# Attention in units of eight heads on two row tiles of the array, with only own blocks of q loaded and the first group written as one list

## The chip, the cores and the metric

The kernel runs on one core of a Trainium2 chip. The metric is the device time of one execution in microseconds. Three timed runs of the kernel before gave 860.01 us in the median (857.99 to 861.16). Chances are told against 0.5% of that, 4.3 us, about what a measurement of this kernel can tell from no change.

## The reference

Three stages follow one another, all in float32.

```python
# attention: B, H, S, D = 4, 8, 576, 64
scores = q @ k.T / 8
# heads 0..3: 0 <= i - j < 32;  heads 4..7: 0 <= i - j < 128 and (i - j) % 4 == 0; else -1e9
attn = softmax(scores);  x = attn @ v            # then x becomes 2304 tokens x 512
# first MLP, d_ff = 2048
h = x @ w_in;  x = (h - tanh(h)) @ w_out
# second MLP, d_ff = 1024
x = (((x @ w1) * (x @ w2)) @ w3) @ w_out
```

A dilated head is a plain window of 32 once its tokens are sorted by their place modulo four, so all heads have a window of 32 keys, and a block of 32 queries needs 64 keys.

## The kernel before, in words

**Numbers.** Weights come from the host as 64-bit floats and are turned into float32 on the chip: one load on SP's queue (L100, tile `st`), `Abs` on ACT (L105), four VectorE instructions on the bits (L110, L114, L120, L123), then a high part on ACT (L128) and a low part on GpSimd (L129). This is called the conversion of a weight below. `tick()` does one step of such a pipeline. The large products are three passes of high and low parts (`mm3`, L415, and `st_y`, L492).

**Attention.** A unit is one batch, one type (plain or dilated), and one of three stretches of 192 queries: 24 units of four heads, two pairs of heads in each. The host lays q out as `qz`: for each pair of heads 128 rows, where a block's 128 columns hold the 64 queries of the first head in the upper 64 rows, those of the second in the lower 64 rows, and zeros elsewhere. So one product over 128 rows gives the scores of one head, though half of its rows are zeros. A unit goes through these steps: `load_q` (one DMA for k, one for q), `load_v` (two DMAs, or four in the first stretch), `at_scores` (one bf16 product that writes the mask, L283, then 24 products in four column tiles of 32, L293), `at_max` and `at_norm` on VectorE, `at_exp` on ACT, the scaling by the sum on GpSimd (L318), three transposes (`at_T`, L326), two copies into a block-diagonal buffer `pb` (L333), `at_pv` (12 products of 64 moving columns, L353), and the high and low part of the result in X (L369, L370).

**First MLP.** The 16 blocks of d_ff are worked off in groups of 3, 4, 4 and 5. In a group, a step is one block for one tile of tokens: `st_h`, tanh on ACT (L449), `h - tanh(h)` on VectorE (L455), its high part on ACT (L457) and low part (L464, on GpSimd in the first group, on VectorE later), and in the next step `st_y`, whose four results are added to Y (L503, L505, L507). In the first group six tiles of 256 tokens and two of 384 are used, later four of 512 and one of 256.

**Order.** Each engine works off its instructions in the order in which the program issues them. `start_up` does the attention of the first batch (six units), with 24 warming products ahead and one per unit. After that, `attn_slot` does one more step of the attention's pipeline for every 1.33 (first six steps) or 1 steps of the first group, so that its products stand between those of the MLP. Every DMA of the attention and of the weights is issued by SP, in one row, and the program gives the DMAs eight semaphores in turn, so that an issue waits until the transfer eight places ahead of it has landed.

The conversions of a group's weights stand in the steps by `tick()`: after the step's VectorE work and after the sums into Y.

Of the kernel before, what the change touches and what calls it, by code (L numbers as in the profile page):

```python
# [15 lines left out]
PS, PT, PX, TE, PH = 2, 1, 2, 2, 1  # L16
GS = (3, 4, 4, 5)
RF = 1.0
WU, WC = 24, 512
NW, NL = 16, 18  # L20
TS = [512] * 4 + [256]
TC, GP, YE = 3, 1, 2
# [14 lines left out]
NB_P = 2  # L37
# [6 lines left out]
KC = DM // 128  # L44


@with_exitstack
def attn_moe_kernel(
# [78 lines left out]
    def cv_split(a, hi, lo):  # L127
        nc.scalar.activation(out=hi, in_=a.bitcast(F32), func=ACTF.Copy)  # L128
        nc.gpsimd.tensor_tensor(out=lo, in0=a.bitcast(F32), in1=hi.bitcast(F32), op=ALU.subtract)  # L129


    W = {}
    queue = deque()
    for c in range(NFC):
        queue.append((("in", c), w_in[c]))
        queue.append((("out", c), w_out[c]))
# [18 lines left out]
    def tick():  # L155

        if bitsed:
            key, a = bitsed[0]
            if len(free) - (reserve[0] if key[0] in ("w1", "w2") else 0) >= 2:
                bitsed.popleft()  # L160
                hi, lo = free.popleft(), free.popleft()
                cv_split(a, hi, lo)
                W[key] = (hi, lo)
        if absed and not bitsed:
            key, st, a = absed.popleft()
            cv_bits(st, a)
            bitsed.append((key, a))
        prefetch()
        if loaded and not absed:
            key, st = loaded.popleft()  # L170
            absed.append((key, st, cv_abs(st)))

# [14 lines left out]
    units = [(b, ty, g) for b in range(B) for ty in (0, 1) for g in range(NG)]  # L187
    PB = 2 * NG
# [5 lines left out]
    def open_attn():  # L194
        st = ExitStack()
        attn_pools["stack"] = st
        one = st.enter_context(tc.tile_pool(name="att", bufs=1))
        attn_pools["pb"] = one.tile([128, NB_P, TU, 4, 2, HQ], F32, name="pb")
        attn_pools["kv"] = st.enter_context(tc.tile_pool(name="kv", bufs=3))
        attn_pools["pp"] = st.enter_context(tc.tile_pool(name="pp", bufs=3))  # L200
        attn_pools["sm"] = st.enter_context(tc.tile_pool(name="sm", bufs=4))
        attn_pools["psS"] = st.enter_context(tc.tile_pool(name="psS", bufs=PS, space=PSUM))
        attn_pools["psT"] = st.enter_context(tc.tile_pool(name="psT", bufs=PT, space=PSUM))
        attn_pools["psX"] = st.enter_context(tc.tile_pool(name="psX", bufs=PX, space=PSUM))

        for e in range(2):
            nc.gpsimd.memset(attn_pools["pb"][64 * e:64 * e + 64, :, :, :, 1 - e], 0.0)
        m = one.tile([128, 6, HW], F32, name="m")
        for j in range(4):
            r = slice(HQ * j, HQ * j + HQ)  # L210
            nc.scalar.dma_start(out=m[r, 1:], in_=masks[r, 1:, 32 * (j % 2):32 * (j % 2) + HW])
        nc.scalar.dma_start(out=m[:, 0], in_=masks[:, 0, :HW])
        nc.scalar.dma_start(out=id_sb, in_=ident)
        attn_pools["m"] = m

    def prep_masks():
        m = attn_pools["m"]

        def put(to, src, eng):
            shape = [128, (to.stop - to.start - 1) // (to.step or 1) + 1, HW]  # L220
            if src.shape[1] != shape[1]:
                src = src.to_broadcast(shape)
            if eng:
                nc.scalar.activation(out=mask_sb[:, to], in_=src, func=ACTF.Copy)
            else:
                nc.vector.tensor_copy(out=mask_sb[:, to], in_=src)

        nc.vector.tensor_copy(out=id16_sb, in_=id_sb)
        put(slice(9, 10), m[:, 0:1], 0)
        put(slice(10, 13), m[:, 1:2], 0)  # L230
        put(slice(0, 1), m[:, 0:1], 1)
        put(slice(1, 6, 2), m[:, 1:2], 1)
        put(slice(2, 7, 2), m[:, 2:5], 1)
        put(slice(7, 8), m[:, 5:6], 1)
        put(slice(8, 9), m[:, 1:2], 1)
# [8 lines left out]
    def load_q(n):  # L244
        if n < len(units):
            b, ty, g = units[n]
            k0, k1 = KS[TU * g], KS[TU * g + TU - 1] + KW
            k = attn_pools["kv"].tile([128, 2, TU * QT + 32], F32, tag="k", name="k")
            nc.sync.dma_start(
                out=k[:, :, :k1 - k0], in_=kT[b, 2 * ty:2 * ty + 2, :, k0:k1].rearrange("e p k -> p e k")  # L250
            )
            q = attn_pools["kv"].tile([128, 2, TU, 2 * QT], F32, tag="q", name="q")
            nc.sync.dma_start(
                out=q, in_=qz[b, 2 * ty:2 * ty + 2, :, TU * g:TU * g + TU].rearrange("e p t c -> p e t c")
            )
            ks[n] = k, q
# [5 lines left out]
    def load_v(n):  # L262
        if n < len(units):
            b, ty, g = units[n]
            v = attn_pools["kv"].tile([128, 2, TU, 2 * D], F32, tag="v", name="v")
            for e in range(2):

                for t0, t1 in ((0, 1), (1, TU)) if g == 0 else ((0, TU),):
                    src = vt[b, 2 * ty + e, :HW, TU * g + t0:TU * g + t1].rearrange("k t c -> k (t c)")
                    ap = [list(d) for d in src.ap]  # L270
                    step = ap[0][0] * window(TU * g + t0, 1)
                    nc.sync.dma_start(
                        out=v[64 * e:64 * e + 64, :, t0:t1].rearrange("k h t c -> k h (t c)"),
                        in_=bass.AP(tensor=src.tensor, offset=src.offset, ap=[ap[0], [step, 2], ap[1]]),
                    )
            vs[n] = v

    def at_scores(n):
        b, ty, g = units[n]
        k, q = ks.pop(n)  # L280
        ps = attn_pools["psS"].tile([128, TU, 2, HW], F32, tag="s", name="s")
        m0 = (M_DIL if ty else M_PLAIN)[g]
        nc.tensor.matmul(  # L283
            out=ps, lhsT=id16_sb,
            rhs=mask_sb[:, m0:m0 + TU].unsqueeze(2).to_broadcast([128, TU, 2, HW]),
            start=True, stop=False, skip_group_check=True,
        )
        for i in range(TU):
            t = TU * g + i
            for e in range(2):  # L290
                for j in range(4):
                    k0 = KS[t] - KS[TU * g] + window(t, j % 2)
                    nc.tensor.matmul(  # L293
                        out=ps[HQ * j:HQ * j + HQ, i, e], lhsT=q[:, e, i, HQ * j:HQ * j + HQ],
                        rhs=k[:, e, k0:k0 + HW], start=False, stop=(i == TU - 1),
                        skip_group_check=True, tile_position=(0, HQ * j),
                    )
        ms = attn_pools["sm"].tile([128, 2, 2 * TU], F32, tag="ms", name="ms")
        ust[n] = dict(ps=ps.rearrange("p i e k -> p (i e) k"), mx=ms[:, 0], sm=ms[:, 1])

    def at_max(n):
        s = ust[n]
        nc.vector.tensor_reduce(out=s["mx"], in_=s["ps"], axis=AX.X, op=ALU.max)
        s["pm"] = attn_pools["pp"].tile([128, 2 * TU, HW], F32, tag="pm", name="pm")
        nc.vector.tensor_tensor(
            out=s["pm"], in0=s["ps"], in1=s["mx"].unsqueeze(2).to_broadcast([128, 2 * TU, HW]), op=ALU.subtract
        )

    def at_exp(n):
        s = ust[n]  # L310
        nc.scalar.activation(out=s["pm"], in_=s["pm"], func=ACTF.Exp, scale=0.125)

    def at_norm(n):
        s = ust[n]
        nc.vector.tensor_reduce(out=s["sm"], in_=s["pm"], axis=AX.X, op=ALU.add)
        nc.vector.tensor_scalar(out=s["sm"], in0=s["sm"], scalar1=1e-9, scalar2=None, op0=ALU.add)
        nc.vector.reciprocal(out=s["sm"], in_=s["sm"])
        nc.gpsimd.tensor_tensor(  # L318
            out=s["pm"], in0=s["pm"], in1=s["sm"].unsqueeze(2).to_broadcast([128, 2 * TU, HW]), op=ALU.mult
        )  # L320

    def at_T(n):
        s = ust[n]
        pt = attn_pools["psT"].tile([128, TU, 128], F32, tag="t", name="t")
        for i in range(TU):
            nc.tensor.transpose(pt[:, i], s["pm"][:, 2 * i:2 * i + 2].rearrange("p a k -> p (a k)"), id_sb)  # L326
        s["ptp"] = pt

    def at_Tcopy(n):
        s = ust[n]  # L330
        pb = attn_pools["pb"][:, n % NB_P]
        for e in range(2):
            nc.scalar.activation(  # L333
# [37 lines left out]

    LAGN, LAGT, LAGP = 1, 2, 3
    slot = [0]
    first = [0] * 4

    def attn_slot():

# [15 lines left out]
        if on[0]:  # L393
            at_max(n)
# [409 lines left out]
```

## Time and profile before

| | us |
|---|---|
| median of three runs | 860.01 |
| the profiled execution, whole | 861.07 |
| its span, first to last instruction | 859.3 |
| TensorE busy (share of the span) | 819.1 (95%) |
| VectorE busy | 483.9 (56%) |
| ScalarE busy | 293.8 (34%) |
| GpSimd busy | 133.0 (15%) |

The profiled execution is 1.8 us longer than its span, and 1.1 us above the median. The span falls into stages: up to about 40 us the attention of the first batch; then the first group of the first MLP with the other three batches' attention between its steps, up to 174.46 us, where the first product of the second group stands; then the other groups of the first MLP (up to about 511 us) and the second MLP. Matmuls are pipelined, so a busy TensorE is not one at its peak; start-to-start times of its blocks say what a block costs.

### The profile page before, as it was taken

What the parts mean: (1) busy time and instruction counts of PE and PEld (TensorE: products, weight loads), DVE (VectorE), ACT (ScalarE), POOL (GpSimd) and SP (SyncE); (2) the same over time, 40 slices, a digit from 0 to 9 for tenths busy, and PEclk for the clock granted to TensorE, in tenths of its full rate; (3) what the DMA queues carried; (4) which work ended last, traced back from release to release, by engine and by line L of the source; (5) the groups of instructions that cost most, each with busy time, mean ns of one, the idle gap of its engine ahead of it and who ended that gap; (6) DMA issues with size and microseconds to landing.
All of it is one profiled execution on the core that took longest, in us unless ns stands there. A gap on an engine that the chain in (4) does not pass through costs nothing.

```text
span 859.3 us, 13590 instructions
## 1 busy us (share of the span) xinstructions
PE 819.1 (95%) x5568; PEld 688.7 (80%) x5574; DVE 483.9 (56%) x789; ACT 293.8 (34%) x557; POOL 133.0 (15%) x120
## 2 busy tenths in 40 slices
PE   7588999999999999999999979999999999999998
PEld 4477999877789788888888878886788888888897
DVE  5588654888735873378888885577612212222121
ACT  3545655444422432234343333333311211211121
POOL 2243232222100210012211131222100000000000
PEclk9789999999999999999999999999999999999999
DMA  9978851222300320012322322133010010010010
GB/s 258 270 216 237 231 169 39 74 99 98 99 1 6 107 84 1 1 50 99 98 74 74 99 98 73 50 99 109 14 50 1 0 50 1 1 49 1 1 50 25
DMA packets 36511, 67.74 MB, mean 79 GB/s; under 512 B 4320, under 2 KB 24928, under 8 KB 36448
## 3 DMA queue, kind: packets, MB, share of 16 engines
q1 hardware_dynamic: 35456, 66.60, 25.5%
q8 instruction: 44, 0.72, 0.3%
q10 hardware_dynamic: 992, 0.26, 0.1%
q14 instruction: 19, 0.16, 0.1%
HBM read 62.13 MB, written 4.72 MB: 78 GB/s over the span
## 4 chain that ended last, share of the span: by engine, by line
PE 65%; DVE 21%; DMA 6%; ACT 5%; issue 2%; SPq 0%; ACTq 0%; DVEq 0%
PE h L415 37%; PE y L492 14%; PE o L697 10%; DVE a L110 4%; DVE a L114 3%; DVE a L120 3%; DVE a L123 3%; DVE th L455 2%; DVE gs L464 2%; ACT gs L457 2%; DMA st<-in_w 2%; PE x L353 2%; DMA v<-in_vt 2%; PE s L293 1%; DVE Y L507 1%
## 5 line engine op out<-in xcount | busy, mean ns | idle before, releaser
L415 PE MATMUL h<-X,LT 128*128 128x512 f32 (+1 forms) x576 | 131.3, 368 | 0.0
L492 PE MATMUL y<-gs,WG 128*128 128x256 f32 (+2 forms) x648 | 123.3, 338 | 5.0 <-DVE Y L507 3.0
L415 PE MATMUL h<-WG,X 128*128 128x512 f32 (+1 forms) x441 | 120.3, 375 | 0.0
L492 PEld LDWEIGHTS y<-gs,WG 128*128 128x128 f32 x648 | 102.4, 189 | 20.2 <-ACT WG L128 2.2
L415 PEld LDWEIGHTS h<-X,LT 128*128 128x128 f32 x576 | 101.5, 188 | 18.0
L415 PE MATMUL h<-X,WG 128*128 128x256 f32 (+2 forms) x567 | 113.9, 341 | 2.1 <-ACT X L369 1.2
L678 DVE TENSOR_TENSOR a_sb<-h,a_sb 128x512 f32<-128x512 f32 (+1 forms) x40 | 25.5, 638 | 158.5 <-PE h L415 152.3
L415 PEld LDWEIGHTS h<-X,WG 128*128 128x128 f32 x567 | 91.8, 196 | 11.7 <-ACT X L369 1.5
L492 PE MATMUL y<-gs,LT 128*128 128x512 f32 (+1 forms) x420 | 93.9, 373 | 5.7 <-ACT gs L457 4.6
L415 PEld LDWEIGHTS h<-WG,X 128*128 128x128 f32 x441 | 83.2, 189 | 15.2
L492 PEld LDWEIGHTS y<-gs,LT 128*128 128x128 f32 x420 | 74.4, 192 | 20.4 <-ACT gs L457 5.6
L455 DVE TENSOR_TENSOR th<-h,th 128x512 f32<-128x512 f32 (+2 forms) x89 | 52.1, 585 | 66.4 <-ACT th L449 66.3
L105 ACT ACTIVATE a<-st 128x512 f32<-128x512 f32 x72 | 48.5, 673 | 100.4 <-DMA st<-in_w 48.6
L457 ACT ACTIVATE gs<-th 128x512 fp32r<-128x512 f32 (+2 forms) x89 | 49.0, 550 | 92.9 <-DVE th L455 92.9
L449 ACT ACTIVATE th<-h 128x512 f32<-128x512 f32 (+2 forms) x89 | 45.4, 510 | 76.3 <-PE h L415 75.9
L464 DVE TENSOR_TENSOR gs<-th,gs 128x512 fp32r<-128x512 f32 (+2 forms) x71 | 44.9, 632 | 46.2 <-ACT gs L457 45.2
L415 PE MATMUL h<-LT,X 128*128 128x512 f32 (+1 forms) x198 | 60.6, 375 | 0.0
L114 DVE TENSOR_SCALAR a<-a 128x512 uint32<-128x512 uint32 x72 | 58.0, 805 | 2.5
L110 DVE TENSOR_SCALAR a<-a 128x512 f32<-128x512 f32 x72 | 59.0, 819 | 0.5 <-ACT a L105 0.5
L129 POOL TENSOR_TENSOR X<-a,X 128x512 fp32r<-128x512 f32 x26 | 35.6, 1367 | 130.5 <-ACT X L128 119.0
L123 DVE SCALAR_TENSOR_TENSOR a<-st,a 128x512 uint32<-128x512 uint32 x72 | 54.2, 753 | 2.5
L120 DVE SCALAR_TENSOR_TENSOR a<-st,a 128x512 uint32<-128x512 uint32 x72 | 53.6, 744 | 2.4
(69 smaller groups left out, 990.3 us busy)
## 6 DMA issues: line engine op xcount, KB each, us to landing
st<-in_w SPq DMA_DIRECT2D x32, 512.0 KB, 3.4
q<-in_qz SPq DMA_DIRECT2D x24, 384.0 KB, 5.1
st<-in_w_in SPq DMA_DIRECT2D x16, 512.0 KB, 3.5
st<-in_w_out SPq DMA_DIRECT2D x16, 512.0 KB, 3.5
v<-in_vt SPq DMA_DIRECT2D x32, 192.0 KB, 5.3
st<-in_wo SPq DMA_DIRECT2D x8, 512.0 KB, 3.4
k<-in_kT SPq DMA_DIRECT2D x16, 224.0 KB, 5.2
v<-in_vt SPq DMA_DIRECT2D x16, 128.0 KB, 3.6
```

Source lines behind the costliest of these rows:

```text
L105: nc.scalar.activation(out=a.bitcast(F32), in_=st[:, :, 1].bitcast(F32), func=ACTF.Abs)
L110: nc.vector.tensor_scalar(out=a.bitcast(F32), in0=a.bitcast(F32), scalar1=2.0 ** -15, scalar2=CMAX, op0=ALU.max, op1=ALU.min,)
L114: nc.vector.tensor_scalar(out=a, in0=a, scalar1=3, scalar2=0x3FFFFFFF, op0=ALU.logical_shift_left, op1=ALU.bitwise_and,)
L120: nc.vector.scalar_tensor_tensor(out=a, in0=st[:, :, 1], scalar=0xC0000000, in1=a, op0=ALU.bitwise_and, op1=ALU.bitwise_or)
L123: nc.vector.scalar_tensor_tensor(out=a, in0=st[:, :, 0], scalar=29, in1=a, op0=ALU.logical_shift_right, op1=ALU.bitwise_or)
L415: nc.tensor.matmul(out=ps, lhsT=a[sel[0]], rhs=b[sel[1]], start=(i == 0), stop=(i == n - 1), **kw)
L449: nc.scalar.activation(out=th[:, :tn], in_=gst[i][:, :tn], func=ACTF.Tanh)
L455: nc.vector.tensor_tensor(out=th[:, :tn], in0=ps[:, :tn], in1=th[:, :tn], op=ALU.subtract)
L457: nc.scalar.activation(out=gs[:, 0, :tn], in_=th[:, :tn], func=ACTF.Copy)
L464: eng.tensor_tensor(out=gs[:, 1, :tn], in0=th[:, :tn], in1=gs[:, 0, :tn].bitcast(F32), op=ALU.subtract)
L492: nc.tensor.matmul(out=y[k], lhsT=wt[sel[0]][:, 128 * k:128 * k + 128], rhs=gs[:, sel[1], :tn], start=(c == 0 and n == 0 and (not packed o ...
L697: nc.tensor.matmul(out=ps, lhsT=cs[:, e, 128 * m:128 * m + 128], rhs=WW[j][f], start=(j == 0 and n == 0), stop=(j == NJ - 1 and n == 2),)
```

## The change

A unit now has eight heads: both types of a batch and stretch together, 12 units in all. The four heads of the plain type lie on rows 0 to 63 of k and q, those of the dilated type on rows 64 to 127. `load_q` fetches k with one DMA of 64 rows per type, and of q only the blocks that are not zero, with four DMAs of 64 rows per type, in pieces of 64 numbers. `at_scores` puts the type on a row tile of the array (`tile_position=(64 * ty, ...)`), and each type writes a bank of its own. `at_pv` takes the transposed weights as they are, without the block-diagonal buffer: 24 products of 32 moving columns per type in four tiles of 64 x 64 instead of 12 of 64 columns. Max, subtraction, exp and sum go over both types in one instruction from the second batch on. In the first batch the types are worked on apart, and its tiles lie in Y, which is not needed yet.

The attention and the whole first group (eight tiles: seven of 256 tokens, one of 512) stand in one list of words, `ORDER`: a letter for the step, a number for the unit, weight or MLP step, p or d for one type. `q`, `v`, `w` are loads, `s` scores, `T` transposes, `P` the products with v, `h` and `y` those of the MLP, `a b c i o` a conversion. The list holds the conversions of all eight weights of the second group too. In the later groups two blocks of the tile of 256 tokens share one step, and `tick()` stands between the high and the low part of a step, ahead of the low part and of the sums into Y.

```diff
+ORDER = """
+q0p S10 v2p K0 q2p K1 s0p w0 S5 M0p q1p E0p s2p N0p q0d S3 a0 m0p M2p T0p b0 E2p q1d C0p s1p N2p c0
...
-    units = [(b, ty, g) for b in range(B) for ty in (0, 1) for g in range(NG)]
-    PB = 2 * NG
+    units = [(b, g) for b in range(B) for g in range(NG)]
+    PB = NG
...
-            nc.sync.dma_start(
-                out=q, in_=qz[b, 2 * ty:2 * ty + 2, :, TU * g:TU * g + TU].rearrange("e p t c -> p e t c")
-            )
+            for ty in parts:
+                r = slice(64 * ty, 64 * ty + 64)
+                nc.sync.dma_start(
+                    out=k[r, :, :k1 - k0],
+                    in_=kT[b, 2 * ty:2 * ty + 2, :, k0:k1].rearrange("e (h p) k -> p (e h) k", h=2),
+                )
+                for m in range(4):
+                    e, h = divmod(m, 2)
+
+                    nc.sync.dma_start(
+                        out=q[r, e, h],
+                        in_=qz[b, 2 * ty + e, D * h:D * h + D, TU * g:TU * g + TU, QT * h:QT * h + QT],
+                    )
...
+                for ty in parts:
+                    r = slice(64 * ty, 64 * ty + 64)
+                    for j in range(4):
+                        h, half = divmod(j, 2)
+                        k0 = KS[t] - KS[TU * g] + window(t, half)
+                        nc.tensor.matmul(
+                            out=ps[ty][HQ * j:HQ * j + HQ, 2 * i + e],
+                            lhsT=q[r, e, h, i, HQ * half:HQ * half + HQ],
+                            rhs=k[r, 2 * e + h, k0:k0 + HW], start=False, stop=(i == TU - 1),
+                            skip_group_check=True, tile_position=(64 * ty, HQ * j),
+                        )
...
-                nc.tensor.matmul(
-                    out=dst, lhsT=v[:, half, i, D * h:D * h + D],
-                    rhs=pb[:, i, j].rearrange("p a q -> p (a q)"), start=True, stop=True,
-                )
...
+                            nc.tensor.matmul(
+                                out=dst, lhsT=v[64 * e:64 * e + 64, half, i, D * h:D * h + D],
+                                rhs=s["pt"][ty][64 * e:64 * e + 64, i, HQ * j:HQ * j + HQ],
+                                start=True, stop=True, tile_position=(64 * e, 64 * h),
+                            )
...
-        sizes = [256] * 6 + [384] * 2 if g == 0 else TS
+        sizes = TS if g else TS0
...
+            w = 2 if g and tn == 256 else 1
...
+        for i in range(N0, NS + 1):
             if i < NS:
...
+                if i > N0:
+                    settle()
+                    st_h(i)
+                    st_tanh(i)
+                    st_g(i)
+                    st_ghi(i)
+                tick()
+                if i > N0:
+                    st_glo(i)
+            if i > N0:
+                st_y(i - 1)
+                st_evac(i - 1, 0)
+                st_evac(i - 1, 1)
```

Three places show how the order moves. First SP's row of DMA issues, in the middle of the attention: before, a stretch with three loads of k and q, of four heads each.

```order
L249 DMA k<-in_kT 128x2x192
L253 DMA q<-in_qz 128x2x384
L272 DMA v<-in_vt 64x2x128
L272 DMA v<-in_vt 64x2x256
L272 DMA v<-in_vt 64x2x128
L272 DMA v<-in_vt 64x2x256
L249 DMA k<-in_kT 128x2x224
L253 DMA q<-in_qz 128x2x384
L272 DMA v<-in_vt 64x2x384 x2
L249 DMA k<-in_kT 128x2x224
L253 DMA q<-in_qz 128x2x384
```

And now, the loads of unit 10 (k and q of both types) and of v for the dilated type of unit 6, which the list puts right behind them.

```order
L121 DMA st<-in_w_out 128x1024
L306 DMA k<-in_kT 64x4x224
L313 DMA q<-in_qz 64x3x64 x4
L306 DMA k<-in_kT 64x4x224
L313 DMA q<-in_qz 64x3x64 x4
L333 DMA v<-in_vt 64x2x128
L333 DMA v<-in_vt 64x2x256
L333 DMA v<-in_vt 64x2x128
L333 DMA v<-in_vt 64x2x256
```

Four heads took one issue for k and one for q; they now take one and four, and all of them move 64 rows instead of 128.

Second TensorE, in the middle of the first group: before, one slot of the attention between two steps of the MLP.

```order
L415 MATMUL h<-X,WG 128x256 x12
L492 MATMUL y_1095<-gs,WG 128x256 x6
L492 MATMUL y_1096<-gs,WG 128x256 x6
L353 MATMUL x<-pb,v 64x2x32 x12
L283 LDWEIGHTS id_sb
L283 MATMUL s<-mask_sb,id_sb 128x384
L293 MATMUL s<-k,q 32x64 x24
L326 MATMUL t<-id_sb,pm 128x128 x3
L415 MATMUL h<-X,WG 128x256 x12
```

And now, `y9 P7 s10 T8d h11` of the list.

```order
L609 MATMUL y_1892<-gs,WG 128x256 x6
L476 MATMUL x<-p,v 64x8x4 x24
L476 MATMUL x<-p,v 64x32 x24
L389 LDWEIGHTS id_sb
L389 MATMUL s<-mask_sb,id_sb 128x384
L389 LDWEIGHTS id_sb
L389 MATMUL s<-mask_sb,id_sb 128x384
L402 MATMUL s<-k,q 32x64 x48
L447 MATMUL t<-id_sb,pm 128x128 x3
L519 MATMUL h<-X,WG 128x256 x12
```

The products with v stand for both types at once and are twice as many; the scores of both types stand in one block of 48.

Third VectorE in the second group, around the end of a tile: before.

```order
L455 TENSOR_TENSOR th<-h,th 128x512
L464 TENSOR_TENSOR gs<-th,gs 128x512
L507 TENSOR_TENSOR Y<-y_3310,Y 128x256
L507 TENSOR_TENSOR Y<-y_3311,Y 128x256
L507 TENSOR_TENSOR Y<-y_3312,Y 128x256
L507 TENSOR_TENSOR Y<-y_3313,Y 128x256
L110 TENSOR_SCALAR a<-a 128x512
L114 TENSOR_SCALAR a<-a 128x512
L120 SCALAR_TENSOR_TENSOR a<-st,a 128x512
L123 SCALAR_TENSOR_TENSOR a<-st,a 128x512
```

And now.

```order
L567 TENSOR_TENSOR th<-h,th 128x512
L131 TENSOR_SCALAR a<-a 128x512
L135 TENSOR_SCALAR a<-a 128x512
L141 SCALAR_TENSOR_TENSOR a<-st,a 128x512
L144 SCALAR_TENSOR_TENSOR a<-st,a 128x512
L581 TENSOR_TENSOR gs<-th,gs 128x512
L627 TENSOR_TENSOR Y<-y_3679,Y 128x512
L627 TENSOR_TENSOR Y<-y_3680,Y 128x512
L627 TENSOR_TENSOR Y<-y_3681,Y 128x512
L627 TENSOR_TENSOR Y<-y_3682,Y 128x512
```

The four instructions of a conversion moved from behind the sums into Y to a place between the step's difference (`th`) and its low part (`gs`).

## Rows read from the trace of the kernel before

**Rows 1.** Windows: length, busy time of each engine, clock share, DMA share, GB/s.

```profile
0.00:40.00 40.00, 25.21 (x458) 16.60 (x464) 22.07 (x50) 15.48 (x32) 9.90 (x15) 0.88 0.95 265
40.00:87.00 47.00, 39.32 (x759) 34.24 (x758) 38.53 (x77) 26.07 (x56) 18.19 (x19) 0.88 0.81 229
87.00:147.00 60.00, 60.00 (x1063) 55.21 (x1053) 33.60 (x85) 33.99 (x77) 17.56 (x23) 1.00 0.54 153
147.00:174.40 27.40, 25.56 (x150) 24.25 (x145) 21.54 (x33) 11.75 (x24) 7.29 (x6) 1.00 0.23 77
174.40:859.30 684.90, 668.98 (x3158) 558.35 (x3156) 368.18 (x546) 206.46 (x368) 80.04 (x59) 1.00 0.16 51
```

**Rows 2.** Timeline of TensorE, 87 to 93.5 us: start, length, what.

```profile
87.36 1.67 PE L415 MATMUL h<-X,WG 128*128 128x256 f32 x12
88.86 1.60 PE L492 MATMUL y<-gs,WG 128*128 128x256 f32 x12
90.39 0.92 PE L353 MATMUL x<-pb,v 128*64 128x64 f32 x24
91.25 0.34 PE L283 MATMUL s<-mask_sb,id_sb 128*128 128x384 bf16 x1
91.51 0.88 PE L293 MATMUL s<-k,q 128*32 128x64 f32 x48
92.32 0.55 PE L326 MATMUL t<-id_sb,pm 128*128 128x128 f32 x3
92.62 1.08 PE L415 MATMUL h<-X,WG 128*128 128x256 f32 x7
```

**Rows 3.** Timeline of SP, 0 to 70 us: its DMA issues.

```profile
0.74 0.40 SPq L100 DMA_DIRECT2D st<-in_w_in  x1
...
34.12 3.91 SPq L272 DMA_DIRECT2D v<-in_vt  x6
...
64.98 0.54 SPq L249 DMA_DIRECT2D k<-in_kT  x1
65.57 0.47 SPq L253 DMA_DIRECT2D q<-in_qz  x1
```

**Rows 4.** Lines L249, L253, L272, L100, L713: ns min/median/max, first and last start.

```profile
L249 SPq DMA_DIRECT2D k<-in_kT x24: 368/540/546, 1.2 to 119.1; - x24
L253 SPq DMA_DIRECT2D q<-in_qz x24: 367/467/1460, 1.7 to 119.7; - x24
L272 SPq DMA_DIRECT2D v<-in_vt x64: 595/607/1378, 7.4 to 134.2; - x64
L100 SPq DMA_DIRECT2D st<-in_w x32: 327/328/328, 409.3 to 599.6; - x32
DMA to landing us min/median/max: 1.6/2.3/2.7
```

**Rows 5.** Waits of TensorE up to 40 us: total, times, longest.

```profile
PE s L293 <- DMA q<-in_qz: 4.2, 3, 2.7
```

**Rows 6.** DMA queues in the first 10 us: packets, MB, share of 16 engines.

```profile
q1 hardware_dynamic: 1846, 2.39, 68.9%
q10 hardware_dynamic: 992, 0.26, 12.0%
```

**Rows 7.** Waits of TensorE from 174.4 us on.

```profile
PE y L492 <- ACT gs L457: 4.6, 3, 2.8
PE y L492 <- DVE Y L507: 4.1, 5, 1.3
PE o L697 <- ACT cs L680: 2.9, 3, 1.2
```

**Rows 8.** Chain that ended last, two pieces: start, length, what.

```profile
87.60 1.43 PE h L415 x12
...
236.85 2.72 PE h L415 x12
```

**Rows 9.** Timeline of VectorE in the second group, 205 to 218 us.

```profile
204.93 2.48 DVE L507 TENSOR_TENSOR Y<-y,Y 128x512 f32<-128x512 f32 x4
```

More of the change, by code (lines that the diff above doesn't have):

```diff
@@ L171, in tick @@
             absed.append((key, st, cv_abs(st)))
+        if bitsed and not later:
+            split()
     def need(*keys):
@@ L201, in open_attn @@
+        attn_pools["pt"] = st.enter_context(tc.tile_pool(name="pt", bufs=4))
         attn_pools["sm"] = st.enter_context(tc.tile_pool(name="sm", bufs=4))
[L202 to L212, printed above, removed]
+        attn_pools["psS"] = st.enter_context(tc.tile_pool(name="psS", bufs=1, space=PSUM))
+        attn_pools["psT"] = st.enter_context(tc.tile_pool(name="psT", bufs=1, space=PSUM))
+        attn_pools["psX"] = st.enter_context(tc.tile_pool(name="psX", bufs=1, space=PSUM))
@@ L258, in window @@
     def window(t, half):
         return 32 * half if t else 0
[L262 to L282, printed above, removed]
-        nc.tensor.matmul(
[L284 to L287, printed above, removed]
+    def load_v(n, parts=AB):
+        if n < NU:
+            b, g = units[n]
+            for ty in parts:
+                v = home(n, 2 * TU * 2 * D, "vv", "v").rearrange("p (h t c) -> p h t c", h=2, t=TU)
+                for e in range(2):
+                    for t0, t1 in ((0, 1), (1, TU)) if g == 0 else ((0, TU),):
+                        src = vt[b, 2 * ty + e, :HW, TU * g + t0:TU * g + t1].rearrange("k t c -> k (t c)")
+                        ap = [list(d) for d in src.ap]
+                        step = ap[0][0] * window(TU * g + t0, 1)
+                        nc.sync.dma_start(
+                            out=v[64 * e:64 * e + 64, :, t0:t1].rearrange("k h t c -> k h (t c)"),
+                            in_=bass.AP(tensor=src.tensor, offset=src.offset, ap=[ap[0], [step, 2], ap[1]]),
+                        )
+                vs[n, ty] = v
@@ new lines, in attn_moe_kernel, with banks_of, x @@
+    NB = 2 * TU
+    order0 = [(n, ty) for ty in range(2) for n in range(PB)]
+    banks0 = {}
+    def banks_of(n, ty):
+        if n >= PB:
+            s = ust[n]
+            return s["both"][:, ty], lambda: s["xt"][:, ty]
+        m = order0.index((n, ty))
+        if 2 <= m < 4:
+            ps = yA.tile([128, 2, 256], F32, tag=f"y{m - 2}", name=f"s{m}").rearrange("p a c -> p (a c)")
+        else:
+            if m % 4 == 0:
+                banks0["s"] = attn_pools["psS"].tile([128, 2, 512], F32, tag="s", name="s")
+            ps = banks0["s"][:, m % 2]
+        def x():
+            if m % 2 == 0:
+                banks0["x"] = x_tile()
+            return banks0["x"][:, m % 2]
+        return ps, x
@@ L290, in at_scores @@
             for e in range(2):
[L291 to L298, printed above, removed]
@@ L362, in at_evac, with places @@
+    def places(n, ty):
+        b, g = units[n]
+        src = ust[n]["x"][ty]
         dst = [X[:, 4 * ty + part:4 * ty + 4:2, b * S:b * S + S] for part in range(2)]
@@ L460, in st_glo @@
     def st_glo(i):
-        tn = steps[i][3]
+        tn = width(i)
         th, gs = gst[i]
-        eng = nc.gpsimd if "p" not in yB and GP else nc.vector
+        eng = nc.vector if steps[i][0] else nc.gpsimd
         eng.tensor_tensor(
@@ L476, in st_y @@
     def st_y(i):
-        g, ti, t0, tn, c, last = steps[i]
-        need(("out", sum(GS[:g]) + c))
-        wt = W["out", sum(GS[:g]) + c]
-        packed = g == 0 and ti < 6
-        if c == 0:
-            gst["y"] = y_ps(tn)
+        g, ti, t0, tn, cs, last = steps[i]
+        need(*[("out", sum(GS[:g]) + c) for c in cs])
+        packed = g == 0 and tn == 256
+        if cs[0] == 0:
+            gst["y"] = y_ps(tn, packed)
         y = gst["y"]
         gs = gst.pop(i)
-        order = [(n, k) for n in range(3) for k in range(KC)]
@@ new lines, in st_y, with st_evac @@
+            for c in cs:
+                release(W["out", sum(GS[:g]) + c])
+    def st_evac(i, part):
+        g, ti, t0, tn, cs, last = steps[i]
+        if cs[-1] != GS[g] - 1:
+            return
+        y = gst["y"]
+        for k in range(2 * part, 2 * part + 2):
+            dst = Y[:, k, t0:t0 + tn]
+            if g:
+                nc.vector.tensor_tensor(out=dst, in0=y[k], in1=dst, op=ALU.add)
+            elif part == 0:
+                nc.scalar.activation(out=dst, in_=y[k], func=ACTF.Copy)
+            else:
+                nc.vector.tensor_copy(out=dst, in_=y[k])
```

511 lines of the change are left out of this document (261 added, 250 removed).

## The prediction

> **What bounds the kernel now.** I read the windows by stage first [rows 1]. From 87 us to the end TensorE is busy nearly all of the time; up to 87 us it is not: 25 of the first 40 us, 39 of the next 47. So time can be won ahead of 87 us by starting earlier, and behind it only by giving TensorE less. In the first 40 us the DMA engines are busy 95% of the time, at 265 GB/s, and TensorE's longest wait there is for a q tile [rows 5]: that stage is bound by loading. From 40 to 87 us VectorE, busy 38.5 of 47 us, and the loads share the bound.
>
> Next the timeline of TensorE [rows 2], start to start: `h` of 256 tokens costs 1.50, `y` 1.53, products with v 0.86, mask 0.26, scores 0.81, transposes 0.30. A slot of four heads costs 2.23. The chain gives 1.43 for an `h` of 256 next to a `y`, and 2.72 for 512 tokens [rows 8]; I take 1.47 for 256.
>
> Last, SP's row. An issue costs 0.467 for q and 0.540 for k, both over 128 rows, but 0.607 for v, over 64 rows [rows 4]; six v in a row take 3.91, 0.65 each [rows 3]. A weight costs 0.33 (0.38 with the gap, by k to q in rows 3, where 0.54 is followed by 0.05). Such a load lands about 2.3 us after its issue [rows 4].
>
> **SP's issues.** The change trades bytes for issues. Before, all units take 24 k, 24 q and 64 v, 112 issues. Now k is 24, q is 96 (four per type and unit), v 64: 184. The bytes of q fall to half. Nothing but SP issues them, in the list's order. Counted in the list, up to the v that `P6` needs (`v6d`, behind all of `q10`) stand 44 v, 8 weights, and 110 k and q. With x for one k or q, the last issue ends at 0.74 [rows 3] + 44×0.65 + 8×0.38 + 110x = 32.4 + 110x.
>
> No row shows x: q and k over 64 rows with three and four pieces a row don't occur. From below, the 128-row issues: 0.47. From above, v: 0.65 back to back, with two pieces a row; if more pieces cost more, 0.75. The nearest row is v, for its 64 rows, without the gap 0.607; I take 0.62. Then SP is done at 100.6, and with 3 us for landing `P6` starts at 103.6. The waits of an issue on the transfer eight places ahead don't count at this x: eight issues last 5 us, more than a landing.
>
> By the same count up to `v1d` (14 v, 3 weights, 30 k and q) SP ends at 0.74 + 9.1 + 1.1 + 18.6 = 29.6. With landing, `P1d`, its evacuation and the low part (some 2.4) the first `h` stands at about 35; before it stood at about 40. So the start gains some 5 us, but the loads behind it are late again before the list has gone far.
>
> Behind `P6` TensorE has no more loads to wait for. Left until the second group's first `h`: six `P` at 2×0.86 (10.3), two `s` at 2×0.26 + 0.81 (2.7), seven `T` at 0.30 (2.1), 24 `h` and `y` of 256 at 1.47 (35.3), five of 512 at 2.72 (13.6): 64.0, and 3 for stalls. That `h` stands at 170.6; before, it stands at the end of the fourth window, 174.4 [rows 1]: −3.9.
>
> **TensorE's own work.** A pair of units of four heads now costs one block of 48×2 scores, two masks, two sets of transposes and two sets of products with v. In rows 2 the 48 records of scores take 0.81, 17 ns each, and the 24 of products with v 0.86, 36 ns each: four column tiles give half of what two give, so a wave costs some 70 ns however many tiles share it. With both row tiles the waves hold eight, and 96 records take 0.81; if row tiles don't overlap, 1.62. Products with v keep 12 waves, of four instead of two, with half the columns: 0.86 if a wave's time stays, 0.43 if it goes with the columns. I take 0.86. A pair costs 0.52 + 0.81 + 1.72 + 0.60 = 3.65 against 4.46, −0.8; the ends are 0 and −1.7. Over the nine units after the first batch that is −7 us, but in my sum only what lies behind `P6` (in the 64.0) counts, since ahead of it TensorE waits for SP.
>
> The Trainium skill, "TensorEngine Tiling (Array Packing)", section Performance Considerations, says that a small matmul has a fixed overhead of some 60 cycles, so that fewer moving columns do not make it shorter. By it a wave of 32 columns costs as one of 64, my 0.86; by columns alone it would be 0.43, and the rest behind `P6` 6×0.86 = 5.2 shorter.
>
> **VectorE up to the second group.** It is busy 22.07 + 38.53 + 33.60 + 21.54 = 115.7 us up to 174.4 [rows 1]. It now also holds the second group's conversions, while max, subtraction and sum over both types save instructions; I take 120. Spread over 170 us it stays off the path; squeezed into 147 it would be 82% busy, as in 40 to 87 us, where TensorE waited. I count nothing here in the forecast, 5 us in the case below where SP is fast.
>
> **Behind the second group's start.** Its weights are ready, so part of the waits there (4.6 + 4.1 + 2.9 [rows 7]) goes; the shared steps give `tanh` and the high part a longer step to hide behind in the tiles of 256. Against it, `tick()` ahead of the low part and the sums puts the four VectorE instructions of a conversion ahead of the four sums at a tile's end (2.48 for four sums of 512 columns [rows 9]; I take the same 2.5 for the four of a conversion, of the same size): the banks come free later, and where a step of 2.72 [rows 8] is shorter than this TensorE waits. The first could be worth 7, the second could cost 4; I take −3.5.
>
> The Trainium skill, "DMA: Bandwidth & Descriptors", section Rules for kernel authors, says to coalesce many small transfers, and that two transfers to disjoint halves of the partitions are to be one over all 128. That speaks against this edit; the trace agrees as far as 0.65 against 0.47 an issue goes. By it x is at the upper end, which is rival D.
>
> **The sum.** 861.07 − 3.9 − 3.5 = 853.7 for an execution like the profiled one, which was 1.07 above the median of the runs: 852.6, told as 852.
>
> **The rivals.** Each 0.01 of x moves the time by 1.1.
>
> A, the forecast: x from 0.57 to 0.68, 847 to 859.
>
> B: k and q cost as before per issue or little more, x 0.47 to 0.57: 837 to 847. For it: the rows of k and q themselves [rows 4]. Against: these have 128 rows, and v, the one with 64, is dearer.
>
> C: SP is not the bound at all (x below 0.47, or loads that TensorE needs later than I count). Then TensorE and VectorE bound the list: first `h` at 33, then 24 `h` (39.0), 23 `y` (36.3), nine units at 3.65 (32.9), the last mask and transposes 1, and 5 of stalls: 147, so −27 − 3.5 = 830, or 836 with twice the stalls. For it: TensorE is idle 15 + 8 us up to 87 [rows 1]. Against: the count of issues.
>
> D, slower: issues or pieces bind. The four pieces a row of k and three of q cost more than the two of v. x of 0.75 gives `P6` at 117.9, the second group at 185, 868; it is slower than before from x = 0.69 on. Or it is the transfers: in the first 10 us SP's queue (q1) took 68.9% of 16×10 us for 1846 packets, 60 ns each of 1295 bytes, the other 19 ns each of 260 bytes [rows 6]. At 60 ns a piece whatever its size, the 192 pieces of one q take 0.72 on 16 engines, the 256 of one k 0.96, and the mean x is 0.77: 869. At 19 ns they take 0.23 and 0.30 and hide behind the issue; size for size that row is the nearer one.
>
> E, the change does not do what it says: row tiles run one after the other. Two `s` behind `P6` cost 0.8 more each, +1.6: still 854; with C it is +7. It rides on the others and has no time of its own to decide.
>
> **How the numbers follow.** A 47%, B 18%, C 14%, D 21%. Faster by over 0.5% (under 855.7): most of A (37 of 47), all of B and C: 69%. Within: the rest of A, and the part of D under 864.3 (9): 19%. Slower: 12%. A measurement cannot tell less than this 0.5% from no change. The range goes from C's lower half, 832, to the middle of D, 866; what lies outside is some 5% below and 10% above.
>
> **What would show it.** SP's row from 5 to 100 us without a gap, and the median of a k and q issue on it, tells x and so A, B, D; gaps of SP with issues done early say C. TensorE's waits for q, k and v up to `P6`, at about 104, and none for loads after it. The second group's first `h` at 171. A score block of 96 records in 0.81, not 1.62, and `P` in 1.72. In the second group no wait for conversions, and a VectorE row where four sums stand behind a conversion with TensorE waiting for `y`. The forecast is wrong if SP stands idle before 100 us, or if TensorE waits for VectorE, not for loads, between 40 and 104 us.

## The result and the profile after

The changed kernel takes 869.0 us in the median of four runs (868.5 to 870.7), the kernel before 860.6 beside it: 1.0107 times the time, interval 1.0081 to 1.0133. It is 1.1% slower, forecast was 0.9% faster (852, range 832 to 866). The profiled execution took 869.45 us, its span is 867.7.

The windows of the changed kernel, columns as in [rows 1], cut at 195.04, where the second group's first `h` stands now.

```profile
0.00:40.00 40.00, 30.27 (x523) 18.82 (x526) 20.65 (x47) 9.79 (x18) 10.58 (x23) 0.72 0.66 171
40.00:87.00 47.00, 38.46 (x836) 32.08 (x832) 29.10 (x50) 18.26 (x38) 15.55 (x16) 0.80 0.64 167
87.00:147.00 60.00, 45.75 (x1069) 40.95 (x1069) 31.32 (x58) 20.12 (x45) 16.01 (x18) 0.83 0.64 173
147.00:195.04 48.04, 47.64 (x588) 44.30 (x587) 25.79 (x46) 23.54 (x54) 20.67 (x22) 1.00 0.24 74
195.04:867.70 672.66, 663.63 (x3157) 557.68 (x3155) 323.20 (x529) 206.19 (x353) 76.34 (x59) 1.00 0.15 51
```

Two things of opposite sign happened. The second group starts 20.6 us later than in [rows 1] (195.0, not 174.5), and from there to the end 672.7 us pass instead of 684.9, 12.2 fewer. In the first 40 us the DMA engines are now less busy than before (0.66, not 0.95), and TensorE waits there for loads about as long as in [rows 5]. So there it is not the transfers that bind, but their issues.

```profile
PE s L402 <- DMA Y<-in_qz: 4.9, 5, 3.4
```

SP's issues in the changed kernel, by line (ns min/median/max; L313 is q, L306 k, L333 v; L121 is a weight, read up to 130 us):

```profile
L313 SPq DMA_DIRECT2D q<-in_qz x72: 595/611/1427, 36.2 to 128.2; - x72
L306 SPq DMA_DIRECT2D k<-in_kT x18: 595/610/1462, 35.5 to 125.0; - x18
L333 SPq DMA_DIRECT2D v<-in_vt x56: 595/605/1587, 29.6 to 158.0; - x56
L121 SPq DMA_DIRECT2D st<-in_w_in x5: 506/533/598, 8.8 to 128.9; - x5
```

Over 64 rows an issue costs 0.61 in the median, with two pieces a row (v), three (q) or four (k). A weight costs 0.53 here, not the 0.33 of [rows 4]. SP's row, a stretch of it (start, length), ends with `v6d`, the last load that `P6` needs:

```profile
108.85 0.53 SPq L121 DMA_DIRECT2D st<-in_w_in  x1
109.49 1.52 SPq L121 DMA_DIRECT2D st<-in_w_out  x1
111.11 0.60 SPq L306 DMA_DIRECT2D k<-in_kT  x1
111.76 2.58 SPq L313 DMA_DIRECT2D q<-in_qz  x4
114.39 0.61 SPq L306 DMA_DIRECT2D k<-in_kT  x1
115.04 4.00 SPq L313 DMA_DIRECT2D q<-in_qz  x4
119.08 2.56 SPq L333 DMA_DIRECT2D v<-in_vt  x4
```

SP has no pause here but one of 1.3 among the last four of q, and is done with `v6d` at 121.6. TensorE at the same time, with the idle time ahead of a row and its releaser in brackets:

```profile
107.49 1.30 PE L402 MATMUL s<-k,q 64*32 64x64 f32 x72 [0.25 <-DMA q<-in_qz]
115.89 0.90 PE L447 MATMUL t<-id_sb,pm 128*128 128x128 f32 x3 [7.10 <-ACT p L455]
118.41 2.93 PE L519 MATMUL h<-X,WG 128*128 128x256 f32 x12 [1.61 <-DVE th L567]
...
121.63 3.88 PE L609 MATMUL y<-gs,WG 128*128 128x256 f32 x24
125.35 1.60 PE L519 MATMUL h<-X,WG 128*128 128x256 f32 x12
126.88 1.60 PE L476 MATMUL x<-p,v 64*64 64x32 f32 x96
```

The longest wait names ScalarE's copy `p`. ScalarE itself stood:

```profile
114.25 0.66 ACT L126 ACTIVATE a<-st 128x512 f32<-128x512 f32 x1 [10.53 <-DMA st<-in_w_in]
114.82 0.64 ACT L629 ACTIVATE Y<-y 128x256 f32<-128x256 f32 x2
115.34 0.50 ACT L455 ACTIVATE p<-t 128x384 f32<-128x384 f32 x1
```

Its next instruction, `a6` (the `Abs` of a weight), waited for the weight that SP issued only at 108.85, and the copy that frees the transposes' bank stands behind it and two evacuations of Y. So one late row reaches TensorE by two ways, the loads of q and v and the loads of weights. Behind the wait of 7.10 the granted clock is 0.50 (1.2 instead of 2.4 GHz) from 116 to 122, and an `h` of 256 takes 2.93; the one at 125.35, at 1.00 again, takes 1.60, and `P6` stands at 126.88.

`P6` itself waits for nothing. In the chain that ended last it hangs on the second weight, by its `Abs`, the `tanh` behind it on ScalarE (117.53) and the `h` at 118.41:

```profile
109.49 7.45 DMA st<-in_w_out
```

### The profile page after: what moved, and what is told of

Its sections match the earlier page's. It is cut to its first block, busy times and chain, and to the rows that moved or that the text cites. A ratio compares the mean times of both kernels' runs of the same rounds, so it can differ in the third digit from the quotient of the medians.

```text
span 867.7 us, 14652 instructions
## 1 busy us (share of the span) xinstructions
PE 825.8 (95%) x6153; PEld 693.8 (80%) x6153; DVE 430.1 (50%) x728; ACT 277.9 (32%) x507; POOL 139.2 (16%) x136
## 4 chain that ended last, share of the span: by engine, by line
PE 79%; SPq 7%; DMA 5%; DVE 4%; ACT 2%; issue 2%; POOL 0%; ACTq 0%; DVEq 0%; POOLq 0%
PE h L519 46%; PE y L609 21%; PE o L797 10%; SPq L313 4%; SPq L333 2%; DMA st<-in_w 2%; PE x L476 1%; SPq L306 1%; DMA st<-in_w_out 1%; DMA st<-in_w_in 1%; DMA v<-in_vt 1%; DMA Y<-in_kT 1%; DVE a L141 1%; DVE a L135 1%; DVE a L144 1%
## 5 line engine op out<-in xcount | busy, mean ns | idle before, releaser
L609 PE MATMUL y<-gs,WG 128*128 128x512 f32 (+1 forms) x648 | 125.3, 342 | 0.1
L519 PE MATMUL h<-X,WG 128*128 128x256 f32 (+1 forms) x591 | 122.6, 343 | 1.9 <-DVE th L567 1.9
L567 DVE TENSOR_TENSOR th<-h,th 128x512 f32<-128x512 f32 (+1 forms) x83 | 51.3, 618 | 131.1 <-ACT th L561 130.9
L519 PE MATMUL h<-LT,X 128*128 128x512 f32 (+1 forms) x402 | 115.9, 373 | 0.0
L561 ACT ACTIVATE th<-h 128x512 f32<-128x512 f32 (+1 forms) x83 | 44.8, 540 | 137.7 <-PE h L519 137.6
L519 PEld LDWEIGHTS h<-LT,X 128*128 128x128 f32 x402 | 73.5, 188 | 13.3
L519 PE MATMUL h<-WG,X 128*128 128x512 f32 (+1 forms) x225 | 69.2, 375 | 0.0
L574 ACT ACTIVATE gs<-th 128x512 fp32r<-128x512 f32 (+1 forms) x83 | 47.8, 576 | 60.7 <-DVE th L567 56.7
L152 POOL TENSOR_TENSOR WG<-a,WG 128x512 fp32r<-128x512 f32 x27 | 35.1, 1298 | 141.0 <-ACT WG L149 125.6
L797 PE MATMUL o<-X,cs 128*128 128x512 f32 x216 | 52.6, 391 | 1.9 <-ACT cs L780 1.9
```

The lines of the kernel that those rows point to most:

```text
L519: nc.tensor.matmul(out=ps, lhsT=a[sel[0]], rhs=b[sel[1]], start=(start and i == 0), stop=(i == n - 1), **kw)
L561: nc.scalar.activation(out=th[:, :tn], in_=gst[i][:, :tn], func=ACTF.Tanh)
L567: nc.vector.tensor_tensor(out=th[:, :tn], in0=ps[:, :tn], in1=th[:, :tn], op=ALU.subtract)
L574: nc.scalar.activation(out=gs[:, 0, :tn], in_=th[:, :tn], func=ACTF.Copy)
L609: nc.tensor.matmul(out=y[k], lhsT=wt[sel[0]][:, 128 * k:128 * k + 128], rhs=gs[:, sel[1], tn * m:tn * m + tn], start=(cs[m] == 0 and n == ...
L797: nc.tensor.matmul(out=ps, lhsT=cs[:, e, 128 * m:128 * m + 128], rhs=WW[j][f], start=(j == 0 and n == 0), stop=(j == NJ - 1 and n == 2),)
```

## The experiments

Median times in us; the kernel before, run beside each of them, stands at 858.7 to 860.9.

**Issues merged, pieces kept (e1).** k of the host lies as (type, dim) by (pair, head), q as one block of 128 rows for each of the four heads.

```diff
-            for ty in parts:
-                r = slice(64 * ty, 64 * ty + 64)
+            rs = [slice(0, 128)] if len(parts) == 2 else [slice(64 * ty, 64 * ty + 64) for ty in parts]
+            for r in rs:
...
-                        in_=qz[b, 2 * ty + e, D * h:D * h + D, TU * g:TU * g + TU, QT * h:QT * h + QT],
+                        in_=qz[b, m, r, TU * g:TU * g + TU, QT * h:QT * h + QT],
```

> The changed kernel, but k and q of both types (units 3 to 11) are loaded together over 128 rows: five issues a unit instead of ten, the same bytes of q, still in pieces of 256 bytes (k's host layout puts both types' rows side by side). Theory S (SP's row of issues is the bound): up to v6d 40 issues fewer at 0.65 plus their share of the long ones, about 0.73 each, so 29 us less on SP's row; P6 moves from 126.9 to between 98 and 105, where TensorE's own work takes over; time 845 (838 to 852) against 869. Theory D2 (the 256-byte pieces bind the transfers): pieces and bytes are the same, so the time stays, 866 to 870.

843.9, ratio to before 0.982 (0.980 to 0.985), as theory S said. SP is done with `v6d` at 93.9, `P6` stands at 102.0, and the second group starts at 170.4. Same bytes and pieces, half the issues of k and q from the fourth unit on: 25 us. SP's row was the bound, and the pieces were not. (An issue now covers 128 rows, not 64, so count and rows changed together; what SP's row costs by both is in its times.)

```profile
L309 SPq DMA_DIRECT2D q<-in_qz x36: 479/487/1335, 35.6 to 97.8; - x36
```

For q an issue of twice the rows is cheaper (0.487), as in [rows 4]; one of k, with four pieces a row, still costs 0.60.

**One issue each for q and k (e2).**

```diff
-                for m in range(4):
...
+                nc.sync.dma_start(out=q[r].rearrange("p e h t c -> p (e h t c)"), in_=qz[b, g, r])
```

> The changed kernel, but the host lays out the own blocks of q so that a unit's q is one DMA with 3072 bytes in a row, and k one DMA, both over 128 rows from unit 3 on and over 64 rows per type in the first batch: two issues where ten stood. Theory S: SP's row up to v6d falls from 162 issues to 80, it is no longer the bound, and the first group is bound by TensorE, VectorE and ScalarE: 830 to 842. If S holds only for the count, e1 and this differ by less than 10 us; if the pieces cost too (D2), this one gains over 20 us and e1 next to nothing.

840.5, ratio 0.979 (0.977 to 0.981); second group at 164.9. Another 3.5 us for 42 issues up to `v6d`. SP is no longer the bound: it is done with `v6d` at 86.7, `P6` stands at 97.8, and up to 130 us SP waits most for VectorE to free a weight's tile:

```profile
SPq L121 <- DVE a L144: 40.9, 6, 21.1
```

**The conversion out of ScalarE's way (e3).** Words of the list:

```diff
-E8 q10 G6 N8 a6 h7 k6 Y5 Z5 C7p m8p s9 a7 b6 m8d t7 v6d g7 T7d c6 G7 h8 k7 C7d q11 M9 i6
+E8 q10 G6 N8 h7 k6 Y5 Z5 C7p m8p s9 m8d t7 v6d g7 T7d G7 h8 k7 C7d q11 M9 a6 b6 c6 a7 i6
```

> The changed kernel, with four words of the list moved: a6, b6, c6 and a7 (the first two weights of the second group) stand behind M9 instead of ahead of h7 to g7, so that ScalarE's Abs no longer waits for a weight ahead of the copy that TensorE's transposes need. Theory S: the wait of 7.1 us at 116 goes, but P6 cannot start before v6d has landed (issued up to 121.7, so about 124.6 against 126.9): 867 (866 to 869). Theory R (the Abs in ScalarE's row is itself the cause): the wait and the slow clock behind it go, 7 to 9 us: 860 to 862.

870.1 (869.2 to 870.5), just above what theory S said. The wait moved, the time stayed:

```profile
118.98 2.93 PE L519 MATMUL h<-X,WG 128*128 128x256 f32 x12 [4.45 <-DVE th L567]
121.84 2.13 PE L476 MATMUL x<-p,v 64*64 64x32 f32 x68
124.23 1.06 PE L476 MATMUL x<-p,v 64*64 64x32 f32 x28 [0.26 <-DMA v<-in_vt]
...
138.42 2.93 PE L519 MATMUL h<-X,WG 128*128 128x256 f32 x12 [3.98 <-DVE th L567]
```

`P6` runs until the last v lands and ends at 125.2, 3 us earlier than in the changed kernel, and still the second group starts at 195.5. Both waits for `th` are again waits for weights: ahead of the `tanh` an `Abs` on ScalarE waited until 116.5 and 135.7 for a load of the same row. So e3 moved the wait by one step and did not take it away, and it does not tell apart what the weights and what the loads of v cost.

**The same count on the kernel before (e9).**

```diff
-            nc.sync.dma_start(
-                out=q, in_=qz[b, 2 * ty:2 * ty + 2, :, TU * g:TU * g + TU].rearrange("e p t c -> p e t c")
-            )
+            for m in range(4):
+                e, r = m // 2, slice(64 * (m % 2), 64 * (m % 2) + 64)
+                nc.sync.dma_start(
+                    out=q[r, e], in_=qz[b, 2 * ty + e, r, TU * g:TU * g + TU],
+                )
```

> The kernel before, with each q load split in four DMAs of 64 rows, one per pair and half of its rows: the bytes, the zeros and the pieces of 1536 bytes stay, 72 issues are added to SP's row. Theory S: each q costs 4x0.65 where it cost 0.47 to 0.51, 2.1 more, 50 us over 24 loads; SP's row of before has some 35 to 40 us of gaps and waits up to 134 us that take up a part: 866 to 880. If SP's row is no bound there: 858 to 861.

869.2, ratio 1.013 (1.010 to 1.016): 72 more issues, as many as the change adds, cost 10.5 us with the bytes and pieces as they were (each issue now over 64 rows). The second group starts at 183.0, 8.5 later than in [rows 1].

**v too (e6).** As e2, and instead of the loops over `e`, `t0`, `t1` in `load_v`:

```diff
+                nc.sync.dma_start(out=v.rearrange("p h t c -> p (h t c)"), in_=vt[b, g, ty])
```

> e2 (two issues a unit for k and q), and v laid out by the host so that a unit's v is one DMA of 128 rows and 3072 bytes a row per type, instead of two or four of 64 rows. Up to v6d another 28 issues go from SP's row. Theory S: in e2 SP's row is no longer the bound behind 40 us, so this gives 0 to 4 us: 836 to 841. If SP still bound e2 at the dearer v: 28 issues at 0.7, so up to 15 us: 825 to 832.

838.6, ratio 0.976 (0.974 to 0.978), the fastest here, not told apart from e2.

**Row tiles in turns or apart (e8).** As e2, and in `at_scores`:

```diff
-        for i in range(TU):
-            t = TU * g + i
-            for e in range(2):
-                for ty in parts:
+        for ty in parts:
+            for i in range(TU):
+                t = TU * g + i
+                for e in range(2):
```

> e2, with the 48 score products of the plain type ahead of the 48 of the dilated type, where they stand in turns of four. In e2 a block of 96 takes 1.11 to 1.20. If the row tiles run side by side only where products of both types are neighbours (theory E's price): the block goes to 2x0.81 = 1.62, 0.45 more for each of twelve units, and TensorE is the bound there: 844 to 847 against 840.5. If a block costs what its 96 instructions cost, whichever tiles they use: no change, 839 to 842.

A block in e2, then in e8:

```profile
63.37 1.17 PE L393 MATMUL s<-k,q 64*32 64x64 f32 x96
```

```profile
93.32 1.44 PE L393 MATMUL s<-k,q 64*32 64x64 f32 x96
```

843.5, ratio 0.982 (0.979 to 0.984): the interval touches that of e2, so the time decides nothing. The block does: 0.27 longer. Row tiles do overlap, but only in part: a block in turns costs 1.17, not the 0.81 that I took.

**The 12 us behind the second group's start.** Undone singly in the changed kernel: the place of `tick()` (e4), the shared steps (e7) and the split in the same `tick()` (e10).

```diff
-                tick()
-                if i > N0:
                     st_glo(i)
...
+            if i < NS:
+                tick()
```

```diff
-            w = 2 if g and tn == 256 else 1
+            w = 1
```

```diff
-        if bitsed and not later:
-            split()
```

Put on the kernel before: the place (e5), place and split (e11, `tick(True)`, which ends with the split), and all three (e12, with the changed kernel's `st_h`, `st_y` and `w`).

```diff
+                if g:
+                    tick()
                 st_glo(i)
...
-            if g or i < 3 or i >= 18 or i % TE == 0:
+            if g == 0 and (i < 3 or i >= 18 or i % TE == 0):
```

> The changed kernel, with tick() of the later groups behind the sums into Y again, as in the kernel before. Behind the second group's first h the changed kernel is 12.2 us faster than the one before. If the place of tick() gives a part of that, TensorE's waits for the sums (4.1 us before) and for the high part (4.6) come back in part: 872 to 876. If the gain is that of the weights converted early and the shared steps alone, no change: 868 to 870.

> The kernel before, with one edit: from the second group on tick() stands ahead of the step's low part, not behind the sums into Y. Theory T (the place of tick() gives the whole gain behind the second group's first h): e4 lost 11.5 us by the way back, so about 11 here, 847 to 850 against 859, and TensorE's waits for the high part (4.6) and the sums (4.1) are nearly gone. If the gain needs the second group's weights converted in the list or the shared steps too: 854 to 859.

> The changed kernel, with one block a step also in the later groups' tiles of 256 tokens (the shared steps undone). If these give a part of the 12.2 us behind the second group's first h: up to 4 us slower, 871 to 873. If tick() and the weights give it all: 868 to 870.

> The changed kernel, with one line of tick() undone: the high and low part of a weight come with the next tick() again, one step after its four VectorE instructions, as in the kernel before. Theory J (the place of tick() gains only together with this line: with the split in the same tick(), GpSimd's low part falls beside VectorE's gs and sums, and not beside a conversion's instruction, which e5 showed at 1.67 instead of 0.69): the conversions go from 2.4 to 3.3 us, the low part comes late, and the second part loses 10 to 20 us: 879 to 889. Theory T (the place alone matters): 868 to 871.

> The kernel before, with both edits of tick() from the second group on: its place ahead of the low part (as in e5) and the split in the same tick(). Theory J: VectorE's conversions fall from 3.15 to about 2.4 us, the waits behind 174 us go, and the 12 us behind the second group's first h come here too: 846 to 849 against 858.7. If the second group's weights converted early in the list are needed: 853 to 858.

> The kernel before with all three edits of the later groups: tick() ahead of the low part, the split in the same tick(), and two blocks of the tile of 256 tokens in a step. Only the second group's weights still come late, and the attention and the first group are those of before. Undone singly in the changed kernel, the three cost 11.5 (place), 5 (split) and 10 (shared steps); the first two alone made the kernel before 5 slower. If the three need only each other: the 10 to 12 us come, 847 to 850. If they need the second group's weights early, converted by the written list: 854 to 862.

| | median | ratio to before |
|---|---|---|
| the change | 869.0 | 1.011 (1.008 to 1.013) |
| e4, place undone | 880.6 | 1.025 (1.023 to 1.027) |
| e7, shared steps undone | 879.3 | 1.023 (1.021 to 1.025) |
| e10, split undone | 874.1 | 1.017 (1.014 to 1.019) |
| e5, before with place | 869.6 | 1.013 (1.011 to 1.015) |
| e11, before with place and split | 865.1 | 1.006 (1.004 to 1.008) |
| e12, before with all three | 853.8 | 0.992 (0.990 to 0.994) |

Neither T nor J holds as put, and none of the six times lies in a range named ahead of it (e12 misses one by 0.2). Each edit undone costs 5 to 12 us; place, or place and split, alone on the kernel before cost 11 and 5; all three gain 7. In e12's profiled execution 5.1 lie behind the second group's start; the start itself stands 3.3 earlier than in [rows 1], which edits of the later groups do not explain. What is left of the 12, some 7, would be the weights converted early, by difference, not by a run. e10 is a weak form of J: 5 us, not 10 to 20, and a conversion takes 3.05.

What TensorE waits for behind the second group's start shows what the edits do to each other. In the kernel before it is 11.6, mostly for the high part and the sums [rows 7]. In e5, then e12, and in the changed kernel:

```profile
PE y L492 <- DVE gs L464: 7.7, 9, 2.6
```

```profile
PE y L510 <- DVE gs L482: 1.6, 1, 1.6
```

```profile
PE o L797 <- ACT cs L780: 3.9, 2, 2.0
PE y L609 <- DVE gs L581: 0.9, 1, 0.9
```

With the new place the low part stands behind a conversion, and TensorE waits for it instead: 7.7 in e5, still 6.8 with the split too (e11), and 5.5 in the changed kernel without the shared steps (e7). With them it is 1.6 and 0.9. So the place takes away the waits for the high part, and the shared steps take away most of what the place brings. The changed kernel waits 4.8 in all, 6.8 less than before; the other 5 of the 12 lie in TensorE's busy time (669.0 to 663.6) and no run explains them. (e12 waits 3.6 once at its second group's first `y`, for the evacuation of Y on ScalarE, which neither the kernel before nor the changed one does.)

The conversions themselves became shorter. Three of VectorE's four instructions from 200 us on, before (busy us, mean ns behind the bar; the fourth keeps its 692):

```profile
L110 DVE TENSOR_SCALAR a<-a 128x512 f32<-128x512 f32 x54 | 46.6, 863 | 0.0
L114 DVE TENSOR_SCALAR a<-a 128x512 uint32<-128x512 uint32 x54 | 45.4, 841 | 1.8
L120 DVE SCALAR_TENSOR_TENSOR a<-st,a 128x512 uint32<-128x512 uint32 x54 | 40.7, 754 | 1.9
```

And after:

```profile
L141 DVE SCALAR_TENSOR_TENSOR a<-st,a 128x512 uint32<-128x512 uint32 x58 | 48.6, 837 | 2.0
L135 DVE TENSOR_SCALAR a<-a 128x512 uint32<-128x512 uint32 x58 | 24.8, 427 | 2.0
L131 DVE TENSOR_SCALAR a<-a 128x512 f32<-128x512 f32 x58 | 24.6, 424 | 0.0
```

3.15 us a conversion become 2.38. That alone gains nothing: in e4 a conversion takes 2.39, and the time is 11.6 longer. In the kernel before GpSimd's low part (L129) starts at 211.52, and L110 at 211.57 takes 1.53 instead of 0.42; in e5 it falls beside L123:

```profile
211.57 1.53 DVE L110 TENSOR_SCALAR a<-a 128x512 f32<-128x512 f32 x1
```

```profile
205.95 1.67 DVE L123 SCALAR_TENSOR_TENSOR a<-st,a 128x512 uint32<-128x512 uint32 x1
```

With the split in the same `tick()` GpSimd begins right behind VectorE's low part (in the changed kernel at 224.09 behind 223.94) and mostly works beside the sums, which keep their 0.68. The Trainium skill, "Advanced Engine Details and Errata", section VectorE Performance Modes, says that VectorE's two-port modes and GpSimd share a port and block each other. For L110 the trace agrees, by 1.1 us; L123 reads two tensors, and no row here shows in which mode it ran.

## Why the prediction was wrong

**The step that failed** is "With x for one k or q ... I take 0.62" and, in the same paragraph, "The waits of an issue on the transfer eight places ahead don't count at this x". The mechanism and the count (162 issues up to `v6d`) were right; the price of the row was too low. It ended at 121.6, not 100.6. Those 21 us are: 4.9 of base price (0.65 an issue with its gap of 0.04 for k and q, a weight 0.51 to 0.60 without the gap instead of 0.33); 9.9 of long issues, 14 that took 0.85 to 1.59 where 0.61 is usual; 6.2 of gaps beyond 0.04, of which 4.2 are waits on transfers ahead. The two longest of those, in SP's own waits up to 130 us:

```profile
SPq L333 <- DMA st<-in_w_in: 2.1, 1, 2.1
SPq L313 <- DMA st<-in_w_out: 1.3, 1, 1.3
```

The waits were put at nothing by a misread row. The landing of 2.3 in [rows 4] is that of the stores of the result (L713, from 630 us on), not of a load. The loads of k, q and v landed after 4.7, 5.1 and 4.2 in the median of the kernel before, and the longest took 8.8 to 9.6; for k:

```profile
DMA to landing us min/median/max: 2.6/4.7/9.6
```

So eight issues, some 5 us, last no longer than a usual landing. In the changed kernel k, q and v land after some 4, 2.8 and 3.8, a weight after 6.3 in the median of those up to 130 us (7.5 at most), and both waits above are on weights. The long issues stood in [rows 4], as maxima of 1.46 and 1.38, and I took medians.

**From `P6` to the second group the working held.** `P6` was 23.3 us late, and from it to the second group's `h` 68.2 us passed (67 forecast): 24.4 late in all. Behind that the change gains 12.2, not 3.5, so 8.7 better. 853.7 + 24.4 − 8.7 = 869.4, the profiled 869.45. The way to `P6` was not quite the one that I put down: it did not wait for `v6d`, but for a weight of the same row, as shown above. Nor did the start gain 5 us: SP is done with `v1d` at 35.5, not 29.6, and the first `h` stands at 47.0, not 35 (39.6 before).

**Rival D** had the right time (868; told like my 852 it is 867) by a price of 0.75, and the wrong reasons: over 64 rows an issue costs 0.61 with two, three or four pieces, and e1 kept the pieces and gained 25 us. That it came close is luck. I gave it 21%, against A's 47%.

**The 12.2 behind the second group.** I counted `tick()`'s new place as a cost of up to 4, by late sums. Alone it does cost, 11 in e5, but by the late low part; in the changed kernel, with the shared steps, undoing it costs 12. Place, or place and split, lose without the shared steps, which no row of before could show.

**TensorE's own work.** `P` costs 1.53 for both types (1.72 taken, 0.86 by columns): a wave takes 64 ns, where one of twice the columns took 72. The Trainium skill, "TensorEngine Tiling (Array Packing)", section Performance Considerations, says that fewer moving columns do not make a small product shorter, and the trace nearly agrees. Scores cost 1.17 in e2 (0.81 taken, 1.62 the bound).

**Case C** was too low too: e2 takes SP out of the way, and the second group starts at 164.9, not 147. There the DMA engines are busy 0.98 of the first 40 us again, and TensorE waits 10.7 us for what the profile calls issue (below).

The Trainium skill, "DMA: Bandwidth & Descriptors", section Rules for kernel authors, was weighed and set aside by me: coalesce, and no two transfers to halves of the partitions. e1, which loads k and q over all 128 partitions, shows its price here: 25 us.

## What to carry to other kernels

Halving the bytes of a load gained nothing here, because it cost 72 more issues on a row that had no room for them. Count the issues on the queue that carries them, at their mean price with the long ones and the waits, not at the median, and put the result beside the time that the consumer needs them. Check of which line a row is before a term rests on it. Rows of a queue reach further than their data: a weight late by the same row stopped ScalarE, and through it the transposes. Where an edit moves the longest wait away, look whether the same late row stops the next step; here it did, and nothing was gained.

## What the runs showed of the hardware

Each of the 14 long issues on SP up to 121.6 begins within 0.5 us of the begin of a packet on a queue of kind instruction (16 KB, about 1 us; one of 8 KB), and 13 of them end 0.37 to 0.41 us behind that packet's end. The one packet of 16 KB in this stretch without a long issue (at 32.4) begins in a wait of SP. The page has 48 such packets on the one queue:

```profile
q8 instruction: 48, 0.79, 0.4%
```

TensorE shows something like it in e2, in blocks of 96 small products:

```profile
57.93 1.14 PE L393 MATMUL s<-k,q 64*32 64x64 f32 x92
60.54 0.30 PE L393 MATMUL s<-k,q 64*32 64x64 f32 x4 [1.47 <-issue]
...
67.21 1.08 PE L467 MATMUL x<-p,v 64*64 64x32 f32 x32 [2.42 <-issue]
```

Packets of this kind begin at 57.7, 60.0 and 65.0, though the wait of 2.42 ends 1.3 behind the end of its packet. By waits of TensorE up to 175 us this is 10.3 us in e2's scores and products with v:

```profile
PE x L467 <- issue: 5.9, 5, 2.4
PE s L393 <- issue: 4.4, 3, 2.0
```

That fetching code makes both waits was not tried by a run; it is a coincidence in time, in every long issue of the changed kernel up to `v6d`. If it is the cause, more and smaller instructions cost twice, on TensorE and on SP; that is not shown.
